# Attention, experts and a feed-forward layer in one kernel: the second head pair packed, and the order of early transfers changed

## The chip, the cores and the metric

One core of one Trainium2 chip runs the whole program. The metric is the device time of one execution in microseconds; three executions of the kernel before took 860.30, 859.90 and 860.27 us, median 860.27.

## The reference

Causal attention with a decay bias, then a mixture of eight experts that picks one per token, then a dense layer with a squared ReLU. All in float32.

```python
# attention: q, k, v of shape (4 batches, 8 heads, 576 tokens, 64), s of shape (4, 8, 576)
scores = (q @ k^T) / sqrt(64)
cum = cumsum(max(s, 0))
scores = where(causal, -1e9, scores + minimum(-(cum[i] - cum[j]), 0))
x = softmax(scores) @ v                       # then (2304 tokens, 512)
# experts: each token goes to the one with the largest logit
e = argmax(x @ w_gate);  gate = softmax(x @ w_gate)[e];  eom = sigmoid(x @ w_output_gate)
y[token] = gate * eom[e] * (relu(x @ w1[e]) @ w2[e])
# dense layer
out = (relu(y @ w_in) ** 2) @ w_out           # (2304, 512)
```

## The kernel before

The 32 heads are worked through as 16 pairs, two heads at a time. A pair's scores are split into seven units by blocks of 128 query rows (`order` at line 46: blocks 0 and 1 of both heads, then single blocks, last the tail of both heads, the "last rows"). For each unit TensorE computes scores, VectorE adds the mask and finds the row minimum, ScalarE takes the exponential, TensorE transposes the result, VectorE or ScalarE copies it out of PSUM, and later TensorE multiplies by the values. The experts and the dense layer follow and take most of the run.

To keep float32 precision, q and k are each split into a high and a low part (`qk_hi` on ScalarE, `qk_lo` on VectorE, from a transpose in PSUM by `qk_pe` on TensorE). A pair's tiles `sta` and `stb` hold four slots of 576 columns on 128 rows: q high, k high, q low, k low. The decay bias comes in as extra rows that multiply cumulative sums.

There are two ways to form the scores, chosen in `emit_s` (line 618). The first `ND` = 2 pairs are *unpacked*: three products for the split q and k, and a fourth with `cum_q` and `cum_k` for the bias. From the third pair on, pairs are *packed*: a head's 64 rows are put beside copies of its high parts and the cumulative sums, in the other 64 rows, so that two products give the same sum. That packing needs, for each pair, three instructions on GpSimd (`copy_b`: two copies and a memset), and four transfers started from SP: a small load of the cumulative sums for the second head (`load_aug`), a move of 64 rows from `sta` to `stb` (`spread_b`), a move inside `sta` (`spread_a`), and the small load for the first head. `spread_a` overwrites rows 64 to 127 of slot 0, which `spread_b` reads:

```python
def spread_b(pp): move(b[0:64, 0::3, 0:S], a[64:128, 0:2, 0:S])
def spread_a(pp): move(a[64:128, 0::3, 0:S], a[0:64, 0:2, 0:S])
```

The order of all this is written as a list of tasks with times, in units of a pair's seventh (`at(key, function, ...)`, line 217). The list is sorted by time and then issued; each engine, and each DMA queue, runs its own instructions in that order. Pair `pp` (counted from 0 in the code) starts its units at 7 `pp`; its first scores are put 2.85 ahead of that. With pairs counted from 0, SP's order before is: q and k of 2, q and k of 3, the gate weights (four small loads, line 1221), q and k of 4, v of 2, small load and `spread_b` of 2, q and k of 5, `spread_a` and small load of 2, v of 3, two stores of pair 0's result, small load and `spread_b` of 3, q and k of 6, `spread_a` of 3. Fetching q and k of a pair (`load_qk`, line 506) is six transfers, v is three (`load_v`).

Ahead of the first scores, TensorE runs eight idle products of 512 columns (`warm`, line 1120) and six more between the first pair's transposes. The q and k of the second pair are transposed between units of the first pair, with the offset `q1` (lines 86 and 1253). `init_rest` (line 1206) sets up token numbers on VectorE and loads the gate weights.

Of the kernel before, what the change touches and what calls it, by code (L numbers as in the profile page):

```python
# [12 lines left out]
F32 = mybir.dt.float32  # L13
# [5 lines left out]
AF = mybir.ActivationFunctionType  # L19
ALU = mybir.AluOpType  # L20
# [4 lines left out]
P = 128  # L25
# [4 lines left out]
K_ = dict(  # L30
    S=3,
    O=0,
    pbufs=4,
    NO=5,
    od=[-1.86, -0.33],
    lorder=[0, 2, 11, 10, 3, 1, 4],
    lvact=[[0], [1], [0], [1], [1], [0], [1, 0]],
    lpv=[[7.65, 7.66], [4.06, 5.56, 6.05, 6.9, 7.45]],
    we=1.93,
    wz=1.0,  # L40
    ring=['o', 't', 'o', 'o', 't', 's'],
# [10 lines left out]
    ldqk=-16.83,  # L52
    ldv=-3.41,
    scq=-4.19,
    sck=-5.35,
    qk=[-3.45, -2.16, -1.89],
    qkh=0.61,
    qkl=0.65,
    dup=-2.9,
    dupa=0.6,  # L60
# [7 lines left out]
    sx=2.42,  # L68
    w0=6.88,
    wld=2.9,  # L70
    wm=(8, 2, 4, 10, 7, 5, 2, 1, 4),
    cvb=0.4,
    ext=4.4,
    exs=5.6,
# [8 lines left out]
    xt0=2.2,  # L83
    xt1=1.3,
    hv=0.9,
    q1=4.32,
)


# [1 line left out]
def attention_moe_ffn_kernel(  # L91
# [14 lines left out]
    nc = tc.nc  # L106
    B, H, S, D = q.shape
    NT, DM = out.shape
    E = w_gate.shape[1]
# [4 lines left out]
    SP = NB * P  # L114
    HP = H // 2
    NPAIR = B * HP
    ND = 2
    NO = K_['NO']
    MC = NT // P
    CAPS = [352, 320, 304, 304, 288, 288, 272, 256]  # L120
# [6 lines left out]
    scale = 1.0 / float(D) ** 0.5  # L127
# [45 lines left out]
    def new_half(pool, key, slot):  # L173
        halves[key] = pool.tile([P, 2, 4096], F32R, tag=slot, name=slot)
# [42 lines left out]
    def at(key, fn, *args):  # L217
        tasks.append((key, len(tasks), fn, args))
# [232 lines left out]
    with tc.manual_schedule():  # L451
        with ExitStack() as actx:
# [37 lines left out]
            def bank(r):  # L490
                if r == "s":
                    return ps_s.tile([P, 512], F32, tag="s", name="s")
                if r == "o":
                    return ps_o.tile([P, 512], F32, tag=o_tag, name=o_tag)
                return ps_t.tile([P, 512], F32, tag="t", name="t")
# [46 lines left out]
            qk_ps = {}  # L542

            def qk_pe(pp, part):
                ps = qk_ps[pp, part] = bank(K_["ring"][part])
                if part < 2:
                    t = raw_q[pp][:, part * QM:(part + 1) * QM]
                    for c in range(NB - 1):
                        nc.tensor.transpose(ps[:, c * P:(c + 1) * P], t[:, c * P:(c + 1) * P], ident)
                else:  # L550
                    nc.tensor.transpose(ps[:, 0:2 * TAIL], raw_q.pop(pp)[:, 2 * QM:], ident)
# [556 lines left out]
            with tc.tile_pool(name="prep", bufs=1) as prep:  # L1108
# [50 lines left out]
                for a in range(2):  # L1159
                    nc.gpsimd.memset(rs_t[a], 1.0)  # L1160
                for a in range(2):
                    nc.gpsimd.memset(st_b[a][0:64, 1].bitcast(F32), 0.0)
                nc.gpsimd.memset(carry, 0.0)
                nc.gpsimd.memset(carryb, 0.0)
                nc.gpsimd.memset(tbl, 0.0)
                nc.gpsimd.memset(wp, 0.0)
                nc.gpsimd.memset(st_a[1][64:128, 0:3:2].bitcast(F32), 0.0)
                nc.gpsimd.memset(st_b[1][0:64, 0:3:2].bitcast(F32), 0.0)
                load_qk(1)
                load_v(0)  # L1170
                for part in range(3):
# [5 lines left out]
                        qk_lo(0, part)  # L1177
                qk_lo(0, 2)
                for r in range(2 * ND):
                    if r < ND:  # L1180
                        nc.scalar.activation(
                            out=cum_q[:, r], in_=cum_r.bitcast(F32), func=AF.Copy, scale=sel[:, r:r + 1])
                    else:
                        nc.gpsimd.tensor_scalar(
                            out=cum_q[:, r], in0=cum_r.bitcast(F32), scalar1=sel[:, r:r + 1], scalar2=None,
                            op0=ALU.mult)
                nc.scalar.copy(out=tri, in_=mt)
                nc.scalar.copy(out=iota_r, in_=ii)
                nc.scalar.copy(out=iota8, in_=ii[:, 0:E])
                nc.scalar.copy(out=iota8p, in_=ii[:, E:2 * E])  # L1190
                nc.sync.dma_start(out=aug_d[0].rearrange("c r t -> (c r) t"), in_=cum_k.bitcast(F32))
                nc.sync.dma_start(
                    out=aug_d[1, 0:2].rearrange("c r t -> (c r) t"), in_=cum_r[0:2 * NH].bitcast(F32))
# [12 lines left out]
            def init_rest():  # L1206
                for t in oT + [lgT]:
                    nc.gpsimd.memset(t[:, S:SP], 0.0)
                nc.vector.tensor_scalar(out=tok[:, :, :, 0], in0=ij, scalar1=-1.0, scalar2=None, op0=ALU.add)
                nc.vector.tensor_copy(out=erow, in_=iota8)  # L1210
                nc.vector.tensor_scalar(out=key0, in0=iota8, scalar1=-1.0, scalar2=7.0, op0=ALU.mult, op1=ALU.add)
                nc.vector.memset(key0[:, 0:1], 1.0e6)
                nc.vector.tensor_single_scalar(out=ik, in_=ij, scalar=6, op=ALU.logical_shift_right)
                nc.vector.tensor_scalar(
                    out=idab[:, :, :, 0], in0=ik, scalar1=64.0, scalar2=None, op0=ALU.mult)
                nc.vector.tensor_single_scalar(out=ij, in_=ij, scalar=63, op=ALU.bitwise_and)
                nc.vector.tensor_copy(out=idab[:, :, :, 1], in_=ij)
                nc.vector.memset(idab[TAIL:P, :, NB - 1], 0.0)
                for hd in range(2):
                    for i, w in enumerate((w_gate, w_ogate)):  # L1220
                        nc.sync.dma_start(
                            out=wp[64 * hd:64 * hd + 64, :, 16 * hd + 8 * i:16 * hd + 8 * i + 8],
                            in_=w.rearrange("(j h p) e -> h p j e", h=2, p=64)[hd])
# [4 lines left out]
                oT.extend(more[:, a] for a in range(NO - 2))  # L1228

            at(0.3, init_rest)  # L1230
            new_half(wpool1, (0, "a"), "w0")
            new_half(wpool1, (0, "b"), "w1")

# [2 lines left out]
            at(NU * ND + 0.5, init_spare)  # L1236

            def early(pp):
                return min(NU, 3 * max(pp - ND, 0))

            for pp in range(NPAIR):
                base = NU * pp
                t0 = base - NU
                if pp >= 2:
                    at(max(t0 + K_["ldqk"] - early(pp), t0 - 2 * NU + K_["scq"] - early(pp - 2) + 0.2), load_qk, pp)
                    at(t0 + K_["ldv"], load_v, pp)
                if pp >= 1:
                    if pp >= ND:
                        at(t0 + K_["sck"] - early(pp), scale_tail, pp, nc.gpsimd)
                    else:  # L1250
                        at(K_["od"][0], scale_tail, pp, nc.vector)
                    for part in range(3):
                        tq = t0 + K_["qk"][part] - early(pp) + (0 if pp >= ND else K_["q1"])
                        at(tq, qk_pe, pp, part)
                        at(tq + K_["qkh"], qk_hi, pp, part)
                        at(tq + K_["qkl"], qk_lo, pp, part)
                if pp >= ND:
                    tb = t0 + max(K_["dup"], K_["qk"][2] + K_["qkl"] - early(pp) + 0.4)
                    at(tb - 0.05, load_aug, pp, 1)
                    at(tb - 0.04, copy_b, pp)  # L1260
                    at(tb, spread_b, pp)
                    at(tb - K_["dup"] + K_["dupa"], spread_a, pp)
                    at(tb - K_["dup"] + K_["dupa"], load_aug, pp, 0)
                end = pp == NPAIR - 1
                units, vact, pv = (K_["l" * end + nm] for nm in ("order", "vact", "pv"))
                for i, un in enumerate(units):
                    u = base + i
                    at(u - K_["LS"], emit_s, pp, un)
                    at(u - K_["LM"], emit_m, pp, un)
                    at(u - K_["LE"], emit_e, pp, un)  # L1270
                    at(u, emit_t, pp, un)
                    at(u + K_["LV"], emit_v, pp, un, vact[i])
                for half in (1, 0) if end else (0, 1):
                    for jb, tv in enumerate(pv[half]):
                        at(base + tv, emit_pv, pp, half, [jb])
                    tv = base + pv[half][-1]
                    tx = tv + K_["xe"]
                    at(tv + K_["ov"], emit_ov, pp, half, K_["ovact"][half])
                    at(tv + K_["rc"], emit_rc, pp, half)
                    at(tv + K_["xt"], emit_xt, pp, half)  # L1280
                    if end:
                        at(tx, emit_xl, pp, half)
                    at(tx + 0.001, emit_xe, pp, half)
                    if end:
                        at(tx + 0.002, store_x, pp, *((0, 2) if half == 0 else (2, NB - 1)))
                        if half == 1:
                            at(tx + 0.002, store_x, pp, NB - 1, NB)
                if end:
                    for hd in range(2):
                        for half in range(2):  # L1290
                            at(tx + 0.003, emit_xa, pp, half, hd)
                else:
                    at(tv + K_["sx"], store_x, pp, 0, NB - 1)
                    at(tv + K_["sx"], store_x, pp, NB - 1, NB)
# [536 lines left out]
```

## Time and profile before

| | us |
|---|---|
| median of three executions | 860.27 |
| profiled execution | 859.34 |
| span of its instructions | 857.6 |
| TensorE busy | 841.0 |
| VectorE busy | 520.2 |
| ScalarE busy | 453.0 |
| GpSimd busy | 262.3 |

Times in a profile count from the first instruction. A timeline row gives the start and the duration of instructions that were merged (x4 is four of them), and in brackets how long the engine had stood idle before and what released it. SP's rows show how long its queue took to start a transfer, not the transfer. In a table of windows, the busy time of each engine stands beside the length of the stretch. PE is TensorE, DVE VectorE, ACT ScalarE, POOL GpSimd.

### The profile page before, as it was taken

Reading aid. Unit: us, or ns where it says so; the run is one execution under the profiler, and the core shown is the slowest. Engines: PE = TensorE matmul, PEld = TensorE weight load, DVE = VectorE, ACT = ScalarE, POOL = GpSimd, SP = SyncE. Lnnn points to the kernel's source line nnn. Section 1 sums busy time; section 2 is a strip of 40 time slices with the busy share of each in tenths; the row PEclk is TensorE's granted clock in tenths of the full one; section 3 lists DMA queues with packets and bytes.
Section 4 is the critical chain, followed back from the end, with each engine's and each line's share of the span. In section 5 each row is a group of like instructions: output and inputs, shape, how many; then the busy total and the mean of one; then the engine's idle time right before and its main releaser. Section 6 shows DMA issues by size and latency. Waiting matters only on the chain. (4 is left out here: it accounts for less than half of the span.)

```text
span 857.6 us, 15157 instructions
## 1 busy us (share of the span) xinstructions
PE 841.0 (98%) x5412; PEld 747.0 (87%) x5412; DVE 520.2 (61%) x1180; ACT 453.0 (53%) x1012; POOL 262.3 (31%) x304
## 2 busy tenths in 40 slices
PE   8999999999999999999999999999999999999996
PEld 6876777777799999999999999999999999999995
DVE  7667877978777677777976767664233343232221
ACT  7787878988465546665655545443233232232221
POOL 6321344543126566566422232331001011001001
PEclk9999999999999999999999999999999999999998
DMA  7676677753287888999983433321010121001001
GB/s 169 143 161 139 153 180 178 177 130 90 77 272 241 254 244 255 252 282 301 288 242 91 148 120 101 95 89 62 13 62 37 37 75 38 1 1 37 0 1 41
DMA packets 113028, 113.14 MB, mean 132 GB/s; under 512 B 66033, under 2 KB 83953, under 8 KB 112946
## 3 DMA queue, kind: packets, MB, share of 16 engines
q1 hardware_dynamic: 104962, 96.68, 42.0%
q0 software_dynamic: 3664, 9.62, 3.3%
q10 hardware_dynamic: 4320, 5.80, 2.0%
q8 instruction: 45, 0.74, 0.4%
q14 instruction: 37, 0.30, 0.1%
HBM read 80.50 MB, written 23.32 MB: 121 GB/s over the span
## 5 line engine op out<-in xcount | busy, mean ns | idle before, releaser
L1431 PE MATMUL z<-xt,w 128*128 128x384 f32 (+6 forms) x1920 | 329.6, 320 | 0.2 <-DVE h L1442 0.2
L1431 PEld LDWEIGHTS z<-xt,w 128*128 128x128 f32 x1920 | 308.1, 188 | 9.0 <-DVE h L1442 0.4
L1482 PE MATMUL z<-w,h 128*128 128x512 f32 x864 | 214.9, 393 | 0.0
L1482 PEld LDWEIGHTS z<-w,h 128*128 128x128 f32 x864 | 160.8, 188 | 29.3
L1451 DVE SCALAR_TENSOR_TENSOR r<-z,r 128x384 f32<-128x384 f32 x96 | 53.3, 556 | 127.2 <-ACT r L1450 127.0
L1450 ACT ACTIVATE r<-z 128x384 f32<-128x384 f32 x96 | 47.2, 491 | 150.6 <-PE z L1431 148.5
L1473 PE MATMUL z<-h,w 128*128 128x304 f32 (+5 forms) x768 | 111.0, 293 | 0.2 <-issue 0.2
L1473 PEld LDWEIGHTS z<-h,w 128*128 128x128 f32 x768 | 104.0, 189 | 0.7 <-issue 0.4
L1399 POOL TENSOR_TENSOR cvm<-cvm,cva 128x512 f32<-128x512 f32 x32 | 44.5, 1390 | 168.6 <-DVE cva L1395 133.7
L1541 POOL DMA_INDIRECT out_dram<-ysb,tok_m x18 | 17.4, 969 | 245.5 <-ACT ysb L1528 183.2
L1458 DVE TENSOR_TENSOR h<-r,h 128x384 fp32r<-128x384 f32 x96 | 61.0, 636 | 50.3 <-ACT h L1457 47.4
L680 ACT ACTIVATE p<-p,nm 128x128 f32<-128x128 f32 (+3 forms) x144 | 84.2, 590 | 2.6 <-DVE nm L663 2.3
L1457 ACT CAST h<-r 128x384 fp32r<-128x384 f32 x96 | 49.3, 513 | 64.0 <-DVE r L1451 63.7
L663 DVE CUSTOM_DVE_ANT_0 p<-s,mask 128x128 f32<-128x128 f32 (+3 forms) x128 | 59.7, 486 | 28.5 <-PE s L636 27.3
L250 DVE TENSOR_TENSOR w<-stg,w 128x1024 fp32r<-128x1024 f32 x49 | 73.6, 1503 | 5.4 <-ACT w L246 3.0
L696 PE MATMUL t<-ident,p 128*128 128x128 f32 x400 | 69.1, 283 | 3.2 <-DVE sta L580 1.1
L246 ACT CAST w<-stg 128x1024 fp32r<-128x1024 f32 x49 | 51.5, 1051 | 18.2 <-POOL cvm L1400 14.2
L696 PEld LDWEIGHTS t<-ident,p 128*128 128x128 f32 x400 | 44.4, 140 | 19.1 <-ACT p L680 6.2
L597 POOL CAST stb<-sta 64x1152 fp32r<-64x1152 f32 x28 | 31.4, 1149 | 78.7 <-PE s L636 46.4
L1400 POOL TENSOR_TENSOR cvm<-cvs,cvm 128x512 f32<-128x512 f32 x32 | 54.1, 1690 | 2.5
L1442 DVE SCALAR_TENSOR_TENSOR h<-z,h 128x304 fp32r<-128x304 f32 (+5 forms) x64 | 28.4, 445 | 37.4 <-ACT h L1441 29.6
L715 ACT COPY pt<-t 128x512 f32<-128x512 f32 (+1 forms) x94 | 46.9, 514 | 7.3 <-PE t L733 4.1
(242 smaller groups left out, 1043.0 us busy)
## 6 DMA issues: line engine op xcount, KB each, us to landing
stg<-in_moe_w_dram SPq DMA_DIRECT2D x42, 512.0 KB
cv<-in_moe_w_out_dram SPq DMA_DIRECT2D x16, 512.0 KB
stx<-in_moe_w_dram SPq DMA_DIRECT2D x14, 512.0 KB
cv<-in_moe_w_in_dram SPq DMA_DIRECT2D x14, 512.0 KB
xr<-yT_d SPq DMA_DIRECT2D x8, 768.0 KB
qk<-in_q_dram SPq DMA_DIRECT2D x32, 128.0 KB
v<-in_v_dram SPq DMA_DIRECT2D x32, 128.0 KB
stg<-in_moe_w_dram SPq DMA_DIRECT2D x16, 256.0 KB
```

The source lines that it names most:

```text
L246: nc.scalar.copy(out=w_parts(job)[0], in_=raw[job])
L250: nc.vector.tensor_tensor(out=lo, in0=raw.pop(job), in1=hi.bitcast(F32), op=ALU.subtract)
L663: nc.vector.tensor_tensor_reduce(out=dst, in0=src, in1=msk, scale=-1.0, scalar=3.0e38, op0=ALU.add, op1=ALU.min, accum_out=nm[:, c:c + 1])
L680: nc.scalar.activation(out=pt[:, cs], in_=pt[:, cs], func=AF.Exp, scale=-1.0, bias=nm[:, c:c + 1], accum_out=rs[:, r:r + 1])
L696: nc.tensor.transpose(tp[:, i * P:(i + 1) * P], pt[:, j0:j0 + P], ident)
L1400: nc.gpsimd.tensor_tensor(out=m, in0=sq, in1=m, op=ALU.add)
L1431: nc.tensor.matmul(ps[:, 0:n], lhsT=wa[:, zw, kk, fl * P:(fl + 1) * P], rhs=xt[:, zx, kk, 0:n], start=(i == 0), stop=(i == 3 * KD - 1))
L1451: nc.vector.scalar_tensor_tensor(out=gg, in0=ps[:, 0:TT], scalar=0.0, in1=gg, op0=ALU.max, op1=ALU.mult)
L1457: nc.scalar.copy(out=ht[:, 0], in_=gg)
L1458: nc.vector.tensor_tensor(out=ht[:, 1], in0=gg, in1=ht[:, 0].bitcast(F32), op=ALU.subtract)
L1473: nc.tensor.matmul(y_acc[g][d][:, 0:n], lhsT=wb[:, zw, fl, d * P:(d + 1) * P], rhs=ht[:, zh, 0:n], start=(f == 0 and i == 0), stop=(f == n ...
L1482: nc.tensor.matmul(acc, lhsT=ht[:, zh, c * P:(c + 1) * P], rhs=wb[:, zw, fl, :], start=(first and i == 0), stop=(last and i == 2))
```

## The change

With pairs counted from 0: `ND` becomes 1, so that pair 1 is packed as well, with the four transfers and `copy_b` that this needs. Its q and k are transposed ahead of the first pair's first scores, into the two PSUM banks of the tail unit. On SP the order becomes: q and k of 2, small load, `spread_b`, `spread_a` and small load of 1, q and k of 3, v of 2, small load, `spread_b`, `spread_a` and small load of 2, q and k of 4, q and k of 5, the gate weights, v of 3, two stores of pair 0's result, small load and `spread_b` of 3, q and k of 6, `spread_a` of 3. The rest keeps its order. `cum_q` needs two slots instead of four, some memsets go, four casts go from ScalarE to GpSimd, the setting up of token numbers goes from time 0.3 to time 3.0 (`init_ids`, just ahead of the first pair's last unit of scores), and the idle products ahead of the first transposes are 13 instead of 8.

```diff
-    wm=(8, 2, 4, 10, 7, 5, 2, 1, 4),
+    wm=(13, 2, 4, 10, 7, 5, 2, 1, 4),
-    q1=4.32,
+    q1=[[-2.87, -2.84, -2.15], [-2.86, -1.2, -1.1], [-0.8, -0.2, -0.15]],
-    ND = 2
+    ND = 1
             def qk_pe(pp, part):
-                ps = qk_ps[pp, part] = bank(K_["ring"][part])
+                if pp == 1 and part < 2:
+                    if part == 0:
+                        qk_ps[pp] = ps_2.tile([P, 1024], F32, tag="s2", name="s2")
+                    ps = qk_ps[pp][:, 512 * part:512 * part + 512]
+                else:
+                    ps = bank(K_["ring"][part])
+                qk_ps[pp, part] = ps
...
-                    nc.gpsimd.memset(st_b[a][0:64, 1].bitcast(F32), 0.0)
+                    nc.gpsimd.memset(st_b[a][0:64, 1:2 + a].bitcast(F32), 0.0)
-                nc.gpsimd.memset(st_a[1][64:128, 0:3:2].bitcast(F32), 0.0)
-                nc.gpsimd.memset(st_b[1][0:64, 0:3:2].bitcast(F32), 0.0)
                 for r in range(2 * ND):
-                    if r < ND:
-                        nc.scalar.activation(
-                            out=cum_q[:, r], in_=cum_r.bitcast(F32), func=AF.Copy, scale=sel[:, r:r + 1])
-                    else:
-                        nc.gpsimd.tensor_scalar(
-                            out=cum_q[:, r], in0=cum_r.bitcast(F32), scalar1=sel[:, r:r + 1], scalar2=None,
-                            op0=ALU.mult)
-                nc.scalar.copy(out=tri, in_=mt)
+                    nc.scalar.activation(
+                        out=cum_q[:, r], in_=cum_r.bitcast(F32), func=AF.Copy, scale=sel[:, r:r + 1])
+                nc.gpsimd.tensor_copy(out=tri, in_=mt)
...
+            def init_ids():
...
+            def load_wp():
...
             at(0.3, init_rest)
+            at(3.0, init_ids)
+            at(8.5, load_wp)
             def early(pp):
-                return min(NU, 3 * max(pp - ND, 0))
+                return min(NU, 3 * max(pp - 2, 0))
                 if pp >= 2:
-                    at(max(t0 + K_["ldqk"] - early(pp), t0 - 2 * NU + K_["scq"] - early(pp - 2) + 0.2), load_qk, pp)
+                    tq = max(t0 + K_["ldqk"] - early(pp), t0 - 2 * NU + K_["scq"] - early(pp - 2) + 0.2)
+                    at({3: 0.5, 4: 6.7}.get(pp, tq), load_qk, pp)
...
+                        if pp == 1:
+                            for t1, fn in zip(K_["q1"][part], (qk_pe, qk_hi, qk_lo)):
+                                at(t1, fn, pp, part)
+                            continue
                 if pp >= ND:
                     tb = t0 + max(K_["dup"], K_["qk"][2] + K_["qkl"] - early(pp) + 0.4)
-                    at(tb - 0.05, load_aug, pp, 1)
+                    if pp == 1:
+                        tb = K_["q1"][2][2] + 0.05
+                    at(tb - 0.05 if pp > 1 else -0.9, load_aug, pp, 1)
                     at(tb - 0.04, copy_b, pp)
                     at(tb, spread_b, pp)
-                    at(tb - K_["dup"] + K_["dupa"], spread_a, pp)
-                    at(tb - K_["dup"] + K_["dupa"], load_aug, pp, 0)
+                    ta = tb - K_["dup"] + K_["dupa"]
+                    if pp <= 2:
+                        ta = tb + (0.02 if pp == 1 else 0.4)
+                    at(ta, spread_a, pp)
+                    at(ta, load_aug, pp, 0)
```

## Rows read from the trace of the kernel before

**Rows 1.** The page, part 1: busy us, share of span, instructions, of TensorE.

```profile
PE 841.0 (98%) x5412; PEld 747.0 (87%) x5412; DVE 520.2 (61%) x1180; ACT 453.0 (53%) x1012; POOL 262.3 (31%) x304
```

**Rows 2.** Windows: stretch, its length, busy us by engine, clock, DMA share, GB/s.

```profile
22.90:38.30 15.40, 15.40 (x122) 13.26 (x122) 9.78 (x33) 10.96 (x32) 5.57 (x6) 1.00 0.73 156
...
51.10:63.10 12.00, 11.81 (x93) 9.14 (x92) 8.29 (x31) 9.87 (x30) 3.36 (x5) 1.00 0.67 152
```

**Rows 3.** Timeline, first 17 us: start, duration, engine, line, operation, tiles, shape, count, wait.

```profile
1.14 3.60 PE L500 MATMUL s<-onesb 128*128 128x512 bf16 x8 [1.14 <-DVE onesb L1119]
...
6.00 1.08 PE L549 MATMUL t<-ident,qk 128*128 128x128 f32 x4 [1.27 <-DMA qk<-in_q_dram]
...
14.44 0.60 PE L549 MATMUL t<-ident,qk 128*128 128x128 f32 x4
...
16.88 0.63 PE L696 MATMUL t<-ident,p 128*128 128x128 f32 x4 [0.70 <-ACT pt L715]
```

**Rows 4.** Timeline of TensorE, pairs two to four.

```profile
23.04 0.56 PE L636 MATMUL s<-sta 128*128 128x192 f32 x3
...
27.65 0.95 PE L636 MATMUL s<-sta,stb 128*128 128x512 f32 x3
...
28.67 0.60 PE L549 MATMUL t<-ident,qk 128*128 128x128 f32 x4
...
38.37 0.45 PE L636 MATMUL s<-sta 128*128 128x192 f32 x2
...
43.01 0.71 PE L636 MATMUL s<-stb 128*128 128x512 f32 x2
43.56 0.79 PE L696 MATMUL t<-ident,p 128*128 128x128 f32 x4
...
51.16 0.45 PE L636 MATMUL s<-sta 128*128 128x192 f32 x2
```

**Rows 5.** Timeline of SP, whose queue starts the transfers: start, time to issue.

```profile
16.49 1.09 SPq L512 DMA_DIRECT2D qk<-in_q_dram  x2
...
20.18 0.60 SPq L1221 DMA_DIRECT2D wp<-in_moe_w_gate_dram  x1
...
23.03 1.10 SPq L512 DMA_DIRECT2D qk<-in_q_dram  x2
...
26.67 1.14 SPq L527 DMA_DIRECT2D v<-in_v_dram  x2
...
28.56 0.44 SPq L539 DMA_DIRECT2D stb<-aug_d  x1
29.11 0.64 SPq L584 DMA_DIRECT2D stb<-sta  x1
...
33.97 0.62 SPq L584 DMA_DIRECT2D sta<-sta  x1
34.64 0.49 SPq L539 DMA_DIRECT2D sta<-aug_d  x1
35.23 1.46 SPq L527 DMA_DIRECT2D v<-in_v_dram  x2
...
38.95 0.52 SPq L875 DMA_DIRECT2D x_d<-xs  x1
...
40.38 0.62 SPq L584 DMA_DIRECT2D stb<-sta  x1
41.06 1.57 SPq L512 DMA_DIRECT2D qk<-in_q_dram  x2
...
45.26 0.61 SPq L584 DMA_DIRECT2D sta<-sta  x1
```

**Rows 6.** DMA, 30.35 to 32.25 us: packets and their sizes.

```profile
DMA packets 361, 0.35 MB, mean 184 GB/s; under 512 B 233, under 2 KB 233, under 8 KB 361
```

**Rows 7.** Windows at the end of the run.

```profile
849.00:850.00 1.00, 0.99 (x5) 0.49 (x3) 0.43 (x1) 0.00 (x0) 0.64 (x3) 1.00 0.24 90
852.00:853.00 1.00, 0.00 (x0) 0.00 (x0) 0.00 (x0) 0.00 (x0) 0.07 (x1) 0.81 0.55 193
```

More of the change, by code (lines that the diff above doesn't have):

```diff
@@ L1179, in attention_moe_ffn_kernel @@
                 for r in range(2 * ND):
-                    if r < ND:
-                        nc.scalar.activation(
-                            out=cum_q[:, r], in_=cum_r.bitcast(F32), func=AF.Copy, scale=sel[:, r:r + 1])
-                    else:
-                        nc.gpsimd.tensor_scalar(
-                            out=cum_q[:, r], in0=cum_r.bitcast(F32), scalar1=sel[:, r:r + 1], scalar2=None,
-                            op0=ALU.mult)
-                nc.scalar.copy(out=tri, in_=mt)
-                nc.scalar.copy(out=iota_r, in_=ii)
-                nc.scalar.copy(out=iota8, in_=ii[:, 0:E])
-                nc.scalar.copy(out=iota8p, in_=ii[:, E:2 * E])
+                    nc.scalar.activation(
+                        out=cum_q[:, r], in_=cum_r.bitcast(F32), func=AF.Copy, scale=sel[:, r:r + 1])
+                nc.gpsimd.tensor_copy(out=tri, in_=mt)
+                nc.gpsimd.tensor_copy(out=iota_r, in_=ii)
+                nc.gpsimd.tensor_copy(out=iota8, in_=ii[:, 0:E])
+                nc.gpsimd.tensor_copy(out=iota8p, in_=ii[:, E:2 * E])
                 nc.sync.dma_start(out=aug_d[0].rearrange("c r t -> (c r) t"), in_=cum_k.bitcast(F32))
@@ L1244, in attention_moe_ffn_kernel @@
                 if pp >= 2:
-                    at(max(t0 + K_["ldqk"] - early(pp), t0 - 2 * NU + K_["scq"] - early(pp - 2) + 0.2), load_qk, pp)
+                    tq = max(t0 + K_["ldqk"] - early(pp), t0 - 2 * NU + K_["scq"] - early(pp - 2) + 0.2)
+                    at({3: 0.5, 4: 6.7}.get(pp, tq), load_qk, pp)
                     at(t0 + K_["ldv"], load_v, pp)
                 if pp >= 1:
-                    if pp >= ND:
+                    if pp >= 2:
                         at(t0 + K_["sck"] - early(pp), scale_tail, pp, nc.gpsimd)
@@ L1252, in attention_moe_ffn_kernel @@
                     for part in range(3):
-                        tq = t0 + K_["qk"][part] - early(pp) + (0 if pp >= ND else K_["q1"])
+                        if pp == 1:
+                            for t1, fn in zip(K_["q1"][part], (qk_pe, qk_hi, qk_lo)):
+                                at(t1, fn, pp, part)
+                            continue
+                        tq = t0 + K_["qk"][part] - early(pp)
                         at(tq, qk_pe, pp, part)
```

## The prediction, made before the changed kernel had run

> **What bounds the kernel now.** I read the page, the table of windows, the timeline of TensorE, the timeline of SP's queue, and the end of the run. The page gives TensorE 98% of the span [rows 1]. The chain of waits is no help here: it holds only the last stores. In the windows TensorE is busy for all 15.40 us of the stretch in which the second pair is scored, and for 11.81 of 12.00 us two pairs later [rows 2]. So an early shift of TensorE's stream reaches the end unchanged: the end moves as the first score product of the pairs moves. The reader should see in [rows 4] the starts 23.04 (second pair), 38.37 (third), 51.16 (fourth).
>
> The SP rows are the second thing to see [rows 5]. SP starts transfers one after the other, and each start takes about 0.6 us of its queue however early it was planned: six for one pair's q and k take 16.49 to 20.18, 3.69 us. From there to 34.64 the rows follow each other without a break, and the pairs' moves sit in that same queue.
>
> The changed kernel touches only work before some 60 us, so the question is when the fourth pair's first score can start.
>
> **The packing itself.** The second pair loses two of four products in each of 12 segments, 24 in all. A 512-column segment took 27.65 to 28.67, 1.02 us, unpacked and 43.01 to 43.56, 0.55 us, packed [rows 4]: 0.47 us for 1,024 columns. The segments have 192 (2), 256 (2), 512 (2), 384 (2) and 288 (4) columns, 3,840 together, 7,680 in two passes: 7.5 x 0.47 = 3.5 us. From 38.37 - 23.04 = 15.33 us the pair falls to 11.8 us if nothing waits, to 12.0 as in the window two pairs later, and to 12.8 (38.37 to 51.16) at worst. I take 12.1, a gain of 3.2.
>
> **The front.** Five more idle products at 3.60/8 = 0.45 us are 2.25 us, of which the wait from 4.74 to 6.00 covers 1.26: up to 1.0 us later. Nine transposes go ahead of the first score, into that part; four took 1.08 us at 6.00 and 0.60 us at 14.44 [rows 3], so they cost 1.3 to 2.4 us there, partly inside waits, and free 1.3 us later on. The token numbers leave VectorE just ahead of the wait of 0.70 us at 16.88, which should go. ScalarE and VectorE split this pair's q and k in three wide operations instead of six narrower ones; two scalings of the shared rows vanish from GpSimd, which gets the copies for packing and four casts of ScalarE's. All this is bounded between 2 us earlier and 1.5 us later at the second pair's first score, which TensorE would reach between 21 and 24.5; I take 21.5. It decides nothing, for the next part is later than it and does not depend on it.
>
> **SP's queue.** Before, SP issues the fetch of pair 4 (pairs are counted from one here) at 16.49, when nothing has to be waited for. After, the second pair's moves stand there. The first move of a pair (head 2's halves to their own tile) reads the upper rows that the second move overwrites; so SP stands at the second move until the first has landed, with everything behind it: the later fetches, the values, the next pair's moves. Before, a six-part fetch lay between the two moves (29.11 and 33.97) and the wait was free; the change puts them back to back for the second and third pair.
>
> How long one landing takes has no row of its own: the move was issued at 29.11 and its 128 large packets (361 less 233) lie between 30.35 and 32.25 [rows 6]. It is at least 3.1 us; with the completion I take 3.3 (an estimate from that row), the bounds 3.1 and 3.9.
>
> Costs, start to start [rows 5]: small load of the shared rows 0.55 (28.56 to 29.11), first move until landed 3.3, second move 0.67 (33.97 to 34.64), second small load 0.59: 5.1 us for a pair's moves. Fetch of q and k 3.69; of v 1.89 (26.67 to 28.56); gate weights 2.85 (20.18 to 23.03); two stores of x 1.1 (0.52 each and the step between).
>
> From 16.49: second pair's moves until 21.6, fetch of pair 4 until 25.3, v of the third pair 27.2, third pair's moves 32.3, fetches of pairs 5 and 6 39.7, gate weights 42.5, v 44.4, stores 45.5, small load 46.0. Here the first move of pair 4 goes out, at 46.0 instead of 40.38. Behind it stand one more fetch, as before, and then the second move: 41.06 to 45.26 is 4.20, with 0.68 for the first move 4.9. The second move is issued at 50.9 instead of 45.26, and lands at 54.2.
>
> The waits that follow on TensorE: the second pair's second move is issued at 20.4 and landed at 23.7, so its first score starts at 23.7, not 21.5 (queued behind it on TensorE stand the third pair's transposes and what is left of the first pair; the engines that read those wait too). Third pair: first move 27.8, second 31.1, landed 34.4; TensorE is there at 23.7 + 12.1 = 35.8, no wait. The fourth pair would be reached at 48; its halves land at 54.2. TensorE stands for about 6 us. **This is the step that decides**: 54.2 - 51.16 = 3.0 us later than before. Bounds: two landings at 3.1 instead of 3.3 give 2.6; fetches just behind a move take 0.5 longer (41.06 to 45.26 against 3.69), and if that holds for the two behind second moves as well, it is 4.0. I take 3.2. The 3.2 us of the packing are all inside the wait, and so is anything in the front.
>
> Next pair: SP at 52.2, v 54.1, stores 55.2, small load 55.7, first move and fetch 60.6, landed 63.9; TensorE needs it at 66. The queue has caught up by then.
>
> **The clock.** At the end of the run TensorE's last product ended near 850.0 and the granted clock of the slice 852 to 853 is 0.81, from 1.00 to 0.50 within it [rows 7]: some 2.6 us of idleness sufficed. A stand of 6 us is longer, so I expect the fourth pair to begin at the 1.2 GHz level. How long until the full level, the front bounds: products of 512 columns took 0.45 us from 1.14, four transposes 1.08 us at 6.00, and 0.60 at 14.44 [rows 3] (the profile prints the full level from the start, which these durations contradict). Half speed for 3 to 5 us of dense work costs 1.5 to 2.5 us; the bounds are 0 (the clock holds) and 3. I take 1.7.
> The Trainium skill (TensorE: Matmul & The Clock Gate, "HAM oscillation - how this bites in real kernels") says that a wait for a transfer between bursts of products brings the throttle back, and that the next burst starts slow. The last rows show the fall; no row of this kernel shows a burst after one. By that rule the sum is the one above, without it 1.7 us less.
>
> **Sum.** 859.34 (the profiled execution) + 3.2 + 1.7 = 864.2; the median of the runs, 860.27, is 0.9 above the profiled execution, so 865.1 for the median.
>
> **The rivals.**
> 1. *The queue keeps pace.* If SP's second move of pair 4 goes out by 44.7, its halves are there at 48 and TensorE does not stand. For it: SP had some room (two parts of v take 1.46 at 35.23, where they wait, against 1.14 at 26.67), and the fourth pair's second move, issued at 45.26, was there 2.6 us before 51.16. Against: the 5.6 us of lateness are a sum of starts none of which is much shorter in any row. Then the second pair starts at 23.7 instead of 23.04 (+0.7) and runs 12.1 instead of 15.33 (-3.2): 2.5 faster, 856.8, or 857.7 for the median. From an issue before 47.9 on the change is not slower. Chance 0.17.
> The Trainium skill (DMA: Bandwidth & Descriptors, "Issuing engines are not separate DMA queues") speaks for it: the sequencer's time to start a transfer "is usually small relative to the DMA itself". Here the start of six parts takes 3.69 us, which the trace puts against the rule; were starts free, the time would be near 856.
> 2. *The same lateness, and the clock holds* through the wait: 859.34 + 3.2 = 862.5, 863.4 for the median. For it: the fall at the end came after all work was over, and TensorE is only paused here. Against: [rows 7]. Chance 0.16.
> 3. *Half the lateness*: of the 34.4 us from 16.49 to 50.9 some 28 are starts; a tenth less of them brings pair 4's halves to 51.4, 0.2 later than before, and the shorter stand leaves the clock up: 859.5, 860.5 for the median. Chance 0.07.
>
> **How the numbers follow.** Forecast: 0.60, 865.1, its own range 862.5 to 868. To hold 8 in 10 the range takes in rivals 2 and 3 and leaves rival 1 and the highest tail out: 859.5 to 868. A change of under 0.2% (1.7 us) can't be told from none: faster 0.17 (rival 1), same 0.07 (rival 3), slower 0.76.
>
> **What would show it.** Right: in SP's timeline after, gaps of 2 to 3 us between the two moves of the second and third pair, pair 4's first move near 46 and second near 51; on TensorE a wait near 48 that ends with the landing of its tile near 54, a granted clock of 0.5 near it, and before that a second pair of about 12 us. Wrong: pair 4's first score before 50, or a wait there below 2 us; the terms of the sum fall separately (3.69 for a fetch, 3.3 for a landing). If the second pair still takes over 14 us, the packing's 3.5 us is wrong, which would change nothing in the end if pair 4 waits.

## The result, and the profile after

The changed kernel took 868.20 us, median of six executions (866.86 to 869.46); the kernel before took 860.10 (859.86 to 860.30). The ratio is 1.0094, interval 1.0081 to 1.0107: slower by 8.1 us, where 865.1 was forecast. The profiled execution took 868.66 us, span 867.0. Ratios here compare undisturbed runs alone, medians all runs.

The page, part 1, of the kernel after: TensorE's busy time is that of [rows 1] to the tenth, with 19 products fewer. So the 9.4 us that the span grew are idle time of TensorE; in its busy time, five more idle products and products that ran slower made up for the ones that the packing saved.

```profile
PE 841.0 (97%) x5393; PEld 746.8 (86%) x5393; DVE 519.4 (60%) x1177; ACT 450.4 (52%) x1005; POOL 262.4 (30%) x307
```

TensorE's timeline of the kernel after: start, duration, line, operation, and in brackets the idle time before and what ended it.

```profile
1.14 4.77 PE L500 MATMUL s<-onesb 128*128 128x512 bf16 x13 [1.14 <-DVE onesb L1125]
...
25.31 0.71 PE L642 MATMUL s<-sta 128*128 128x192 f32 x2 [4.69 <-DMA sta<-aug_d]
...
39.01 0.45 PE L642 MATMUL s<-sta 128*128 128x192 f32 x2
...
57.87 0.71 PE L642 MATMUL s<-sta 128*128 128x192 f32 x2 [5.83 <-DMA sta<-aug_d]
...
71.70 0.45 PE L642 MATMUL s<-sta 128*128 128x192 f32 x2
```

Behind the idle products of the first row, these are the first scores of the pairs two to five. Against [rows 4] the second is 2.27 us late, the third 0.64 (the packed second pair took 13.70 us instead of 15.33), the fourth 6.71: TensorE stood 5.83 us for the transfer into `sta`. The fifth is 8.51 late, against the first of these two rows of the kernel before (its fifth and sixth pair):

```profile
63.19 0.45 PE L636 MATMUL s<-sta 128*128 128x192 f32 x2
...
77.31 0.45 PE L636 MATMUL s<-sta 128*128 128x192 f32 x2
```

From there the offset stays until the gathered rows of the expert stage, for which TensorE waits 0.8 us instead of 0.2; at the first expert product it is 9.09, and at TensorE's last products 9.07. So 8.5 of the 9.4 us are lost before 72 us.

The windows of the kernel after (columns as in [rows 2]; the last three are granted clock, DMA share, GB/s):

```profile
25.30:28.70 3.40, 3.39 (x16) 3.40 (x17) 1.44 (x6) 0.89 (x2) 0.52 (x1) 0.50 0.72 163
28.70:39.00 10.30, 10.30 (x82) 7.94 (x82) 7.49 (x26) 8.75 (x28) 4.23 (x6) 1.00 0.60 130
...
57.80:62.80 5.00, 4.93 (x24) 4.96 (x24) 2.59 (x11) 2.14 (x8) 0.00 (x0) 0.50 0.81 183
62.80:71.70 8.90, 8.85 (x70) 6.60 (x69) 5.02 (x20) 7.03 (x20) 1.93 (x2) 1.00 0.59 140
```

The second and the fourth pair each begin at the 1.2 GHz level (0.50) behind a wait of some 5 us, and go on at 2.4 GHz (1.00). The fourth pair took 71.70 - 57.87 = 13.83 us, against 12.03 before.

SP's timeline of the kernel after (L539 small load, L590 move, L512 first part of a fetch, L1224 gate weights, L527 values, L877 store):

```profile
16.55 0.45 SPq L539 DMA_DIRECT2D stb<-aug_d  x1
17.10 0.64 SPq L590 DMA_DIRECT2D stb<-sta  x1
21.12 0.62 SPq L590 DMA_DIRECT2D sta<-sta  x1
...
22.37 1.45 SPq L512 DMA_DIRECT2D qk<-in_q_dram  x2
...
26.40 1.14 SPq L527 DMA_DIRECT2D v<-in_v_dram  x2
...
28.62 0.44 SPq L539 DMA_DIRECT2D stb<-aug_d  x1
29.16 0.62 SPq L590 DMA_DIRECT2D stb<-sta  x1
32.44 0.62 SPq L590 DMA_DIRECT2D sta<-sta  x1
...
33.65 1.49 SPq L512 DMA_DIRECT2D qk<-in_q_dram  x2
...
37.77 1.09 SPq L512 DMA_DIRECT2D qk<-in_q_dram  x2
...
41.93 0.61 SPq L1224 DMA_DIRECT2D wp<-in_moe_w_gate_dram  x1
...
44.62 1.44 SPq L527 DMA_DIRECT2D v<-in_v_dram  x2
...
46.90 0.68 SPq L877 DMA_DIRECT2D x_d<-xs  x1
...
48.24 0.44 SPq L539 DMA_DIRECT2D stb<-aug_d  x1
48.78 0.61 SPq L590 DMA_DIRECT2D stb<-sta  x1
...
53.66 0.61 SPq L590 DMA_DIRECT2D sta<-sta  x1
54.32 0.49 SPq L539 DMA_DIRECT2D sta<-aug_d  x1
```

The order is the one that the prediction walked through; the starts follow each other, and the two back-to-back moves stand 4.02 and 3.28 us apart. SP's waits in this stretch (waited for: us in total, times, longest) put 5.9 us of that on the landing of the first move:

```profile
SPq L590 <- DMA stb<-sta: 5.9, 2, 3.3
```

The fourth pair's second move goes out at 53.66, 8.4 us later than the 45.26 of [rows 5].

### The profile page after: what moved, and what is told of

Read it like the earlier page. It is cut to its first block, busy times and chain, and to the rows that moved or that the text cites. A ratio compares the mean times of both kernels' runs of the same rounds, so it can differ in the third digit from the quotient of the medians.

```text
span 867.0 us, 15123 instructions
## 1 busy us (share of the span) xinstructions
PE 841.0 (97%) x5393; PEld 746.8 (86%) x5393; DVE 519.4 (60%) x1177; ACT 450.4 (52%) x1005; POOL 262.4 (30%) x307
## 5 line engine op out<-in xcount | busy, mean ns | idle before, releaser
L642 PE MATMUL s<-sta 128*64 128x288 f32 (+4 forms) x198 | 49.2, 344 | 11.0 <-DMA sta<-aug_d 10.5
L603 POOL CAST stb<-sta 64x1152 fp32r<-64x1152 f32 x30 | 33.6, 1149 | 75.9 <-PE s L642 50.0
```

## The experiments

The theory: the changed order makes SP start the fourth pair's second move late, TensorE stands for it, and the clock falls in that wait. The rivals: the packing or its front costs the time by itself; the clock plays no part; SP's queue is not what sets the start. All edits are to the changed kernel unless said otherwise; pairs count from 0 in code, from 1 in the text.

**1. The fourth pair's moves first.** The fetch of pair 6 goes between its two moves, the fetch of pair 7 and the gate weights behind them.

```diff
-at({3: 0.5, 4: 6.7}.get(pp, tq), load_qk, pp)
+at({3: 0.5, 4: 6.7, 5: 11.12, 6: 14.65}.get(pp, tq), load_qk, pp)
-at(8.5, load_wp)
+at(22.0, load_wp)
```

> The changed kernel, but on SP the fetch of pair 6 stands between the two moves of the fourth pair, the fetch of pair 7 behind them, and the gate weights far behind. Queue theory (SP's order makes the fourth pair late, and nothing else costs): the fourth pair's second move is issued near 46.7 instead of 53.66, its first score starts near 52 without a wait above 1 us, the clock holds there, and the time is 860 (859 to 862). Rival (the packing of the second pair and its own wait are the loss, the fourth pair's wait only collects it): the wait shrinks, but the time stays above 866.

Measured: 862.55 us (860.88 to 866.31), ratio 1.0025 (1.0008 to 1.0041), just above the 859 to 862 that was expected. TensorE's timeline, pairs three to five:

```profile
39.07 0.45 PE L642 MATMUL s<-sta 128*128 128x192 f32 x2
...
51.85 0.45 PE L642 MATMUL s<-sta 128*128 128x192 f32 x2
...
65.47 0.44 PE L642 MATMUL s<-sta 128*128 128x192 f32 x2 [1.33 <-POOL qk L521]
```

The wait ahead of the fourth pair is gone (no bracket behind 51.85), and the clock stays up there; three quarters of the loss went with them (2.1 us left of 8.1). The fifth pair now waits 1.33 us and starts 2.28 late. The row names GpSimd as what ended this wait; the pair's second move on SP went out at 61.47, 4.00 us ahead of the score (4.21 for the fourth pair of the change), so its landing may have ended with it. Which of the two it was is not shown.

**2. The new order without the packing.** The kernel before, with only SP's order from the change:

```diff
+tq = (the time as before)
+at({3: 0.5, 4: 6.7}.get(pp, tq), load_qk, pp)
+at(8.5, load_wp)        # no longer inside init_rest
+ta = tb + 0.4 if pp == 2 else (the time as before)
```

> The kernel before, second pair unpacked, with only the changed order of SP: fetch of pair 4 at 0.5, of pair 5 at 6.7, gate weights at 8.5, the third pair's second move at once behind its first. Queue theory: the fourth pair's second move is issued near 50.4 instead of 45.26, its first score near 54.5 instead of 51.16, and the time is 864 (862 to 867) with no packing in it. Rival (packing is the loss): 860, as before.

Measured: 866.88 us (865.06 to 867.35), ratio 1.0071 (1.0049 to 1.0093). TensorE's timeline, pairs three to five, and the window behind its wait:

```profile
38.38 0.45 PE L636 MATMUL s<-sta 128*128 128x192 f32 x2
...
54.81 0.71 PE L636 MATMUL s<-sta 128*128 128x192 f32 x2 [3.40 <-DMA sta<-aug_d]
...
68.95 0.45 PE L636 MATMUL s<-sta 128*128 128x192 f32 x2
```

```profile
54.80:61.10 6.30, 6.29 (x28) 6.00 (x29) 2.81 (x12) 3.50 (x12) 0.00 (x0) 0.50 0.83 188
```

No pair was packed that was not packed before, and most of the loss is there: the order alone makes the fourth pair 3.65 us late, and the clock adds to 5.76 at the fifth. The products of the packed pair are not what costs the time. (SP stood 3.7 us for ScalarE here ahead of the third pair's first move; in the change, where the second pair's moves come before it, this wait is 0.3.) In the change, with the second pair's moves in the queue as well, the fourth pair's second move goes out 3.17 us later still (53.66 against 50.49 here), and its first score 3.06.

**3. TensorE kept busy in the wait.** 24 idle products of 512 columns ahead of the fourth pair's first score.

```diff
+at(18.14, warm, 24, 512, "s")
```

> The changed kernel with 24 idle products of 512 columns ahead of the fourth pair's first score, in TensorE's wait. Clock theory: the granted clock holds there, the pair from the fourth's first score to the fifth's takes 12.0 us instead of 13.83, the first score itself starts as late as before (57.9), and the time falls by 1.8 to 866.4. Rival (the slow start of the fourth pair is late data, not the clock): 868.2, unchanged.

Measured: 866.20 us (865.12 to 867.83), ratio 1.0068 (1.0044 to 1.0091). TensorE's timeline around the wait (the row at 69.16 is the fifth pair), and the fourth pair's window:

```profile
52.03 5.34 PE L500 MATMUL s<-onesb 128*128 128x512 bf16 x24
57.09 0.48 PE L642 MATMUL s<-sta 128*128 128x192 f32 x2
...
69.16 0.45 PE L642 MATMUL s<-sta 128*128 128x192 f32 x2
```

```profile
57.10:69.10 12.00, 11.81 (x92) 9.15 (x91) 7.50 (x29) 8.89 (x27) 1.87 (x2) 1.00 0.77 174
```

The pair's data are as late as before: the first score comes 4.13 us behind the second move (issued at 52.96, 0.7 us earlier than in the change), against 4.21. From there the pair takes 12.07 us at full clock, 1.76 less than behind an idle wait. That is the clock's price in these two traces, and the rest of the loss is the wait itself. The medians, 866.20 and 868.20, agree with it, but the intervals of the two ratios touch.

**4. A fetch between the second pair's moves,** where it uses SP's stand for the landing.

```diff
-at({3: 0.5, 4: 6.7}.get(pp, tq), load_qk, pp)
+at({2: -0.09, 3: 0.5, 4: 6.7}.get(pp, tq), load_qk, pp)
```

> The changed kernel with the fetch of the third pair put between the second pair's two moves. Queue theory: the first move goes out near 13.9 instead of 17.10, the fetch fills the wait, the second pair's first score starts at 22.5 to 23 instead of 25.31 and the clock holds there; all behind it on SP is about 3 us earlier, so the fourth pair's first score is near 55 instead of 57.87 and the time 865 (863.5 to 866.5). Rival (q and k of the third pair now come too late and give it back): the second pair's first score still at 25 or later, 868.

Measured: 866.81 us (865.22 to 868.30), ratio 1.0062 (1.0038 to 1.0086). The fourth pair started at 56.48, 1.4 us earlier (near 55 was expected), so in the profile SP's stand was partly recovered; the time lies just above the expected range, and its interval overlaps that of the change. The clock fell behind the shorter wait of the second pair too, which I had not expected, and that pair took 15.15 us; since the fourth pair still waits 4.82 us, this costs nothing there. The row and the window:

```profile
23.50 1.06 PE L642 MATMUL s<-sta 128*128 128x192 f32 x2 [2.28 <-DMA sta<-aug_d]
```

```profile
23.20:30.00 6.80, 6.47 (x28) 5.96 (x28) 2.67 (x12) 3.37 (x12) 2.46 (x3) 0.50 0.66 144
```

**5. Eight idle products at the front, as before.**

```diff
-wm=(13, 2, 4, 10, 7, 5, 2, 1, 4),
+wm=(8, 2, 4, 10, 7, 5, 2, 1, 4),
```

> The changed kernel with 8 idle products at the front, as before, instead of 13. Queue theory: the first pair's scores start some 0.7 us later (near 10.5 instead of 9.84) and the clock rises later, but the second pair's first score waits for SP anyway, at 25.3, and the time is that of the changed kernel, 868 (866.5 to 869.5). Rival (the front shifts the whole stream): 0.7 us and more above the changed kernel's runs, and the second pair starts later by as much.

Measured: 867.86 us (866.17 to 870.46), ratio 1.0092 (1.0073 to 1.0110): the time of the change. The second pair began 0.7 us earlier, at 24.62, and the fourth stood 5.71 us all the same. The five added products decide nothing.

**6. All of these orders, and busy waits.** The fetch between the second pair's moves, the later fetches behind the moves that are due, gate weights last, 12 idle products ahead of the second pair.

```diff
+at({2: -0.09, 3: 0.5, 4: 6.2, 5: 11.12, 6: 14.65, 7: 21.65}.get(pp, tq), load_qk, pp)
+at(6.6 if pp == 2 else t0 + K_["ldv"], load_v, pp)
+at(26.0, load_wp)
+at(4.14, warm, 12, 512, "s")
```

> The changed kernel with SP's order mended everywhere: a fetch between the two moves of the second, third and fourth pair, the v of the third pair and the fetches of pairs 7 and 8 behind the moves, the gate weights far behind; and 12 idle products in TensorE's wait ahead of the second pair. Queue theory: first scores near 23.5 (second pair, clock holding), 35.8 (third), 48.5 (fourth), 60.8 (fifth, before 63.19), time 858 (856.5 to 859.5), faster than before: the packing's gain comes out once nothing waits for SP. Rival (the packing gives nothing, as other engines bound a packed second pair): the second pair still takes 15 us and the time is 860 or more.

Measured: 865.98 us (863.97 to 867.72), ratio 1.0060 (1.0044 to 1.0076). Pairs three to five began at 35.84, 48.62 and 60.65, as expected: the last is 2.54 us ahead of the 63.19 of the kernel before, which is what the packing is worth. Then, in TensorE's timeline and the window behind it:

```profile
60.65 0.45 PE L642 MATMUL s<-sta 128*128 128x192 f32 x2
...
74.08 0.64 PE L834 MATMUL t<-oT,wp 128*32 128x256 f32 x2 [4.69 <-DMA wp<-n_moe_w_output_gate_dram]
```

```profile
73.00:79.80 6.80, 5.71 (x31) 3.55 (x32) 1.82 (x5) 2.96 (x8) 0.07 (x1) 0.50 0.61 137
```

The gate weights, started from 69.97 on, are needed here; the wait of 4.69 us and the clock behind it take back more than was won. A miss on the time: I had counted the products to come in the pairs and not the first use of these four loads.

**7. The same without the 12 products.**

```diff
-at(4.14, warm, 12, 512, "s")
```

> The same without the 12 idle products. Clock theory: the clock falls in the wait ahead of the second pair, which then takes 2 to 3 us longer; part of it is hidden in later waits, so the time is 1 to 3 us above the version with the products (859 to 861). Rival (a wait of under 3 us leaves the clock up): the same time within 0.5 us.

Measured: 864.74 us (861.53 to 869.46), ratio 1.0039 (1.0019 to 1.0059); pairs three to five at 35.55, 48.33, 60.36, then the same wait for the gate weights (4.31). Neither expectation came out: the median is 1.2 us below that of experiment 6, and the intervals overlap. The idle wait ahead of the second pair left the clock up in this profile, though it is as long as in experiment 4:

```profile
23.27 0.44 PE L642 MATMUL s<-sta 128*128 128x192 f32 x2 [2.45 <-DMA sta<-aug_d]
```

```profile
23.20:30.00 6.80, 6.73 (x49) 5.32 (x51) 5.63 (x21) 5.59 (x18) 3.60 (x5) 1.00 0.68 143
```

So the second pair took 12.28 us, the packing's worth without a fall.

**8. Experiment 6 with the gate weights started from ScalarE's queue,** early.

```diff
-nc.sync.dma_start(out=wp[...], ...)
+nc.scalar.dma_start(out=wp[...], ...)
-at(26.0, load_wp)
+at(4.13, load_wp)
```

> The version with all orders mended and the 12 idle products, and the four gate-weight loads started from ScalarE's queue in TensorE's wait ahead of the second pair, not from SP behind the sixth pair's fetch, where they came 4.7 us late for the first batch's logits. Queue theory: second to fifth pair's first scores as there (23.0, 35.8, 48.6, 60.7), the sixth at 74.8 instead of 82.1 (before: 77.31), and the time 858 (857 to 859.3), some 2.4 faster than before. Rival (the gain is taken back by a later wait, as SP stays as late as it is through the attention part): 860 or more.

Measured: 860.41 us (859.11 to 863.35), ratio 0.9997 (0.9987 to 1.0008): the time of the kernel before, not below it, as the rival had it. The granted clock is 1.00 in every window from 4.7 to 850 us, and the great waits are gone, but small ones are spread over the pairs that follow:

```profile
62.65 0.44 PE L642 MATMUL s<-sta 128*128 128x192 f32 x2 [0.63 <-DVE pt L723]
...
77.56 0.44 PE L642 MATMUL s<-sta 128*128 128x192 f32 x2 [0.56 <-DMA sta<-aug_d]
```

The fifth pair is 0.54 us ahead of before, the sixth 0.25 behind (77.31). The gain of 2.5 goes in pieces, 0.79 us inside the second pair for a move, 0.63 and 0.56 here, and a transfer into `sta` is again among what TensorE waits for.

**9. The same without the 12 products.**

> The same without the 12 idle products. If the clock held through the wait of 2.4 us ahead of the second pair, as in one look, the time is the same within 0.5 us (858); if it falls in some executions, those are 1 to 3 us longer and the runs spread more widely than with the products.

Measured: 861.34 us (856.46 to 863.61), ratio 1.0001 (0.9986 to 1.0016). No gain either. Single executions spread over 7 us (the kernel before beside them: 859.36 to 862.53), and the lowest had a mean granted clock of 0.998 against 0.993 to 0.995 for the others, so the clock seems to fall in some executions and not in others. In the profiled one (858.40 us) it fell: behind the wait of 2.53 us the stretch from 27 to 30 us is at 0.62, and the second pair took 14.42 us. Even so its sixth pair started at 76.75, 0.56 ahead of the kernel before, so this fall alone does not explain the slower executions.

**10. Only the gate weights taken off SP's queue,** a dose of 2.69 us.

```diff
-nc.sync.dma_start(out=wp[...], ...)
+nc.scalar.dma_start(out=wp[...], ...)
-at(8.5, load_wp)
+at(4.13, load_wp)
```

> The changed kernel with one edit: the four loads of the gate weights are started from ScalarE's queue at time 4.13 instead of from SP's at 8.5. They took 2.69 us of SP's queue ahead of the fourth pair's moves. Theory (SP's starts add up one by one): the fourth pair's second move goes out 2.7 us earlier, near 51.0, its first score starts near 55.2 instead of 57.87, the granted clock still falls there, and the time drops by 2.7 us to 865.5 (864 to 867). Rival (the queue stands for the landings of moves or for the DMA engines, so that what is taken off it in one place is waited for in another): first score of the fourth pair at 57 or later, time 867 to 869.

Measured: 868.69 us (866.08 to 870.39), ratio 1.0086 (1.0058 to 1.0114). In the profile, of SP and then of TensorE:

```profile
40.12 2.12 SPq L512 DMA_DIRECT2D qk<-in_k_dram  x2
...
51.76 0.61 SPq L590 DMA_DIRECT2D sta<-sta  x1
```

```profile
56.03 0.71 PE L642 MATMUL s<-sta 128*128 128x192 f32 x2 [2.37 <-DMA sta<-aug_d]
```

The second move went out 1.90 us earlier instead of 2.7 (at the fetch shown this execution already ran 0.57 us later, and two of its parts took 2.12 us to start, against 1.69 in the change), the first score came 1.84 earlier, and the profiled execution took 866.08, 2.6 us less than that of the change. The wait is shorter by more than that (2.37 instead of 5.83 us), as TensorE itself reached the fourth pair 1.6 us later. The median shows none of it. So the profile bears out that the first score follows SP's second move, but the dose is not repaid in full, and a gain in the time is not shown.

**11. The small load behind the second move, from GpSimd's queue,** for the fourth pair.

```diff
-nc.sync.dma_start(out=st_of(pp)[hd][y0:y0 + 4, 1:3, 0:S]...
+(nc.gpsimd if pp == 3 and hd == 0 else nc.sync).dma_start(out=st_of(pp)[hd][y0:y0 + 4, 1:3, 0:S]...
```

> The changed kernel with one edit: the fourth pair's small load of cumulative sums into sta, which stands behind the second move on SP, is started from GpSimd's queue, so it no longer waits for SP to start the move. It tells which of the two the first score waits for. If the small load (my reading of the waits): first score 3.3 to 3.7 us after the second move's start instead of 4.21, so near 57.2. If the move itself lands that late: 4.2 us as before, first score near 57.9. The time moves by less than 1 us either way.

Measured: 868.25 us (one execution). SP's row of the second move, and TensorE's first two scores of the fourth pair:

```profile
54.03 0.61 SPq L590 DMA_DIRECT2D sta<-sta  x1
```

```profile
56.54 0.50 PE L642 MATMUL s<-sta 128*128 128x192 f32 x1 [3.41 <-DMA sta<-aug_d]
...
57.64 0.53 PE L642 MATMUL s<-sta 128*128 128x192 f32 x1 [0.60 <-DMA sta<-sta]
```

With the small load early, the first product goes, and the second one waits for the move itself: 3.61 us from its start to its use. With the load behind it on SP the first score comes at 4.21. So in this one execution the move's landing is 3.6, and the load behind it costs 0.6 more. The first score came 2.5 us behind the move's start, outside both expectations, as its first product needs the small load alone.

## Why the prediction was right in its mechanism and short in its size

Right, step by step: SP's order and where it stands; a wait of TensorE ahead of the fourth pair (5.83 us measured, about 6 forecast) that ends with the landing in its tile (its cause is as forecast, its length is luck, see below); the clock at 0.50 behind it; a front that decides nothing (experiment 5). Experiment 2 shows that the order does it without the packing, experiment 1 that taking the lateness of the fourth pair away takes the wait and the fall away.

**The step that failed is the term that was called the one that decides:** the fourth pair's halves landing 3.0 us (taken: 3.2) later than 51.16. Measured, its first score is 6.71 later, 3.5 more than taken; with 1.80 instead of 1.7 for the clock and 0.6 at the gathered rows that is 4.2 of the 4.5 us between the profiled execution's 868.66 and the sum's 864.2; the rest lies behind TensorE's last products. (The medians are 3.1 apart, as this profiled execution lay 0.5 above its median and that of before 0.9 below; 868.2 is just above the 868 at which the forecast's own range ended.) It comes from two mis-sized parts. That the wait came out near 6 us all the same is luck: TensorE reached the fourth pair at 52.04 instead of 48, and the first score came at 57.87 instead of 54.2, both some 4 us late.

- *The queue.* From the second pair's small load to the fourth pair's second move I had 34.4 us; it took 37.1 (16.55 to 53.66). By starts: the fetch of pair 4 took 4.03 instead of 3.69 and those of pairs 5 and 6 took 4.12 and 4.16, together 1.24 more; the second pair's moves 5.82 instead of 5.1, all of it in the landing of the first (4.02 instead of 3.3, outside the 3.9 that I gave as a bound); two sets of values 2.22 and 2.28 instead of 1.89, 0.7 more; stores 0.2 more; the third pair's moves (5.03) and the gate weights (2.69) a little less. I had taken the fetch and the values from quick rows (3.69 and 1.89), where the starts waited for nothing, although [rows 5] held a fetch behind a move at 4.20 and two parts of values at 1.46. I had named the half microsecond for fetches behind a move and put 1.0 us on it as a bound only; it was the usual case, and the fetch of pair 6, behind no move, took as long.
- *The last landing.* From the second move's start to the first score I took 3.3 us; it was 4.21. I had left out the small load that stands behind the move on SP, and experiment 11 splits it: 3.61 and 0.6.

The same two parts put the second pair's first score at 25.31 instead of 23.7. The clock fell there too, which I had not forecast, and that pair took 13.70 instead of 12.1; 12.28 in experiment 7, with the clock up, shows that the packing's sum was right to 0.2 us. None of this reaches the end, as the fourth pair waits. The front came out just past its bound on the early side: TensorE was ready for the second pair at 20.62, against 21 to 24.5, and nothing hung on it.

The clock's price, 1.7 forecast, is 1.76 by experiment 3 and 1.80 between the kernels. The 3 to 5 us at half speed behind the forecast had no row of their own in the kernel before; the fourth pair's stretch at 0.50 was 5.0 us long. The Trainium skill (TensorE: Matmul & The Clock Gate, "HAM oscillation - how this bites in real kernels") says that a wait for data between bursts brings the throttle back and the next burst starts slow; the fourth pair's window at 0.50, and the 1.00 of experiment 3 with the wait filled, agree.

Of the rivals, *the queue keeps pace* needed the second move by 44.7; it went at 53.66. Its 2.5 us are real, for experiment 6 had them at the fifth pair, but none of the orders that I tried kept them. *The clock holds* falls by the window; *half the lateness* by both. The Trainium skill (DMA: Bandwidth & Descriptors, "Issuing engines are not separate DMA queues") calls the sequencer's time to start a transfer usually small relative to the transfer itself; here the starts are the queue, 4.1 us for a pair's q and k, and the measurement decides.

Open: whether an order keeps the packing's gain. Experiments 8 and 9 tie with the kernel before; one execution of experiment 9 took 856.46 us, but its median does not. Why the median of experiment 10 did not follow its profile is open too.

## What to carry to other kernels

When instructions are moved into a queue that runs without a break, add up the starts of everything behind them until the next dated use, with durations from rows at the same place in the queue (behind a move, behind a full stretch) and not from the quickest ones, and count what stands between the last transfer and its user. A saving on the bounding engine is worth nothing until the transfer that its next work waits for also comes earlier. An order that mends one due time moves the lateness to the next user, so follow it until the queue has room again.

## What the runs showed of the hardware that was not expected

- A wait of 2.28 us ahead of the second pair was followed by 6.8 us at the 1.2 GHz level in experiment 4, one of 2.45 by none in experiment 7: the length of the wait alone does not tell. In experiment 5 the granted clock was 1.00 through a wait of 3.29 us ahead of the second pair and for 1.4 us of work behind it, and 0.50 from 26.00 to 28.00. So the 2.6 us of idleness that [rows 7] show ahead of the fall at the end did not carry over to that wait.
- The stretches at 0.50 were 3.4 us long in the second pair of the change and 5.0 in its fourth, and about 6.8 us long in experiments 4 and 6; the cost differed with it (13.70 and 15.15 us for the second pair, against 12.28).
- Executions spread, and not only with such waits in the program: 866.86 to 869.46 for the change and 859.86 to 860.30 for the kernel before in the runs beside it, but 859.79 to 867.61 for the kernel before beside experiments 5 to 7. What lengthens single executions is not shown.
- A move of 64 rows inside on-chip memory that was started at 17.10 held up the one that depends on it for 4.02 us, another at 29.16 for 3.28, by a DMA share of 0.48 and 0.51 in the two stretches: the longer one is not the busier one.
